# Value products of an attention and gating kernel: three full query slices for each head pair, the leftover queries in 64x64 tiles, and new instruction orders

## The chip, the cores and the metric

The kernel runs on one core of one Trainium2 chip. A core has a matrix engine (PE, whose weight loads are listed apart as PEld), three engines for elementwise work (DVE, ACT, POOL) and a queue engine, SP, that starts transfers (DMA); ACT and POOL can start transfers too. Each engine works through its own instructions in the order in which they stand in the program, and semaphores make one engine wait for another. The metric is the device time of one execution in microseconds, here the median of three runs.

## The reference, cut to what matters

```python
# q, k, v: (8, 12, 448, 64)
scores = scale * q @ k.T                       # for each of 8 x 12 heads, 448 x 448
m = max(scores, axis=-1); e = exp(scores - m)
attn = e / (sum(e) + exp(-m) + 1e-9)
x = (attn @ v) put together as (8, 448, 768)
proj = x @ w_proj                              # 768 -> 3 * 768
x1, x2, x3 = the three parts of proj
x2 = irfft(rfft(x2, axis=1) * rfft(filter_fft, axis=0))   # along the sequence
out = (x1 * x2 * x3) @ w_out
```

## The kernel before, in words

Exponentials are taken without the maximum, so the divisor is the sum of the exponentials plus 1. A flag tells at the end whether a divisor overflowed, and a branch would then do everything again in a safe way; it isn't taken here.

The work is one long list of tasks, each on one engine, with the tokens that it needs and makes (`add(engine, cost, want, emit, need=, make=, ...)`). A class `Plan` replays the list with its own costs (the numbers in `add`, `LANDING`, `DELAY`, `SWITCH` and others) and emits the tasks in the order of that replay. `plan.ORDER` holds one rank for each task, `plan.BANK` the PSUM banks, `plan.FLIP` those tasks that go to their other engine (`alt`). The order of every engine is therefore a table of numbers. On PE, `fill` puts matmuls on a tile of zeros (`idle`) into spare time of the first 40 us, and `spin` puts some at the very start.

**Attention.** The 12 heads of a batch are 6 head pairs, numbered `i`; two pairs, `lead` (even) and turned (odd), make a block, 24 blocks in all. Keys are cut into three tiles of 128 and a rest of 64.

- `scores(t)`: for t = 1 to 3, four matmuls in 64x64 tiles of the array (two heads by two halves of a key tile), 448 queries wide. `t = 0` does the rest keys of both pairs of a block together.
- `exps(t)`: one activation (ACT) of 128x896 for each; it writes `e` (one of `NE` buffers) or `er` (rest keys, one buffer).
- Value products. The queries stand as weights (up to 128 of them), and `vn` (values with a column of ones, 65 wide) streams. The two pairs of a block share one PSUM bank for each head: 2 x 448 queries are 7 slots of 128. Slot 3 is shared: its first 64 rows are the last 64 queries of `lead`, its other rows the first 64 queries of the turned pair.
  - `out_rest(u)`: the products of the three full key tiles for head `u`, on the whole 128x128 array. Every pair goes through four slices, 4 x 3 = 12 matmuls for each head. The slice in slot 3 is half zeros, which is why `e` has 64 columns of zeros (`pads`) around its 448.
  - `out_rests()`: the rest keys with `er`, 14 matmuls in 64x64 tiles for each pair, for `lead` two more on zeros.
  - Two row halves of the array must not write to one bank at the same time. `lead` writes from one half, the turned pair from the other, so `seen` stands between them: a tiny operation (POOL memset `sinks`, in the first 6 blocks ACT copy `sink`) that waits for the first matmuls of `lead`'s `out_rests`, and for which the turned pair's `out_rests` waits.
- `norm` (DVE) adds 1 to the sums, inverts them and scales, into `xb`.

**Inputs.** Batches 0 and 1 (`staged`) are transposed on PE (`k_turn`, `q_turn`) and copied to `kT` and `qT` by DVE or ACT. The later batches (`loaded`) are cast on POOL and transposed by DMA (SP). The rest keys of batches 0 and 1 are transposed three pairs of columns at a time, one beside each second `k_turn` (`turn0` for the first).

**Dense part.** The projections (L1285, L1187, L1169), the transforms (L1235, L1239, L1331) and the output projection (L1103) are matmuls 113 to 452 wide on the whole array, put between the attention's by `ORDER`.

```python
need=[("e", i), ("ones", b % 2), ("v", i), ("vr", b)] + ([("seen", lead)] if turned else [])   # out_rests before
need=[("ER", i), "pads"] + ([("VU", lead, u)] if turned else [])                               # out_rest before
```

## Time and profile before

| | us |
|---|---|
| median of 3 runs | 367.22 |
| the runs | 367.07, 367.22, 370.21 |
| span of the profiled execution, first to last instruction | 367.4 |
| ACT busy in that span | 240.9 (66%) |
| DVE busy | 275.3 (75%) |
| POOL busy | 129.3 (35%) |
| q loads on the SP queue, issue to landing (median) | 4.2 |
| q loads on the POOL queue, issue to landing (median) | 7.8 |

Of the profiled execution the page gives the span, not a device time of its own; the span is 0.2 us over the median of the runs. In rows of the timeline, the first number is the start in us from the beginning of the span, the second the time from the first start to the last end of the instructions that the row puts together (`x8`: eight of them). In rows of groups, the numbers behind the bar are the busy time in us and the mean ns of one. A matmul's own duration of 190 to 350 ns is mostly its way through the array: the next one starts before it ends, so what a matmul costs PE is the distance from its start to the next start.

### The profile page before, as it was taken

What the parts mean: (1) busy time and instruction counts of PE and PEld (TensorE: products, weight loads), DVE (VectorE), ACT (ScalarE), POOL (GpSimd) and SP (SyncE); (2) the same over time, 40 slices, a digit from 0 to 9 for tenths busy, and PEclk for the clock granted to TensorE, in tenths of its full rate; (3) what the DMA queues carried; (4) which work ended last, traced back from release to release, by engine and by line L of the source; (5) the groups of instructions that cost most, each with busy time, mean ns of one, the idle gap of its engine ahead of it and who ended that gap; (6) DMA issues with size and microseconds to landing.
All of it is one profiled execution on the core that took longest, in us unless ns stands there. A gap on an engine that the chain in (4) does not pass through costs nothing. (4 is left out here: it accounts for less than half of the span.)

```text
span 367.4 us, 10725 instructions
## 1 busy us (share of the span) xinstructions
PE 357.2 (97%) x4312; PEld 214.9 (59%) x4312; DVE 275.3 (75%) x667; ACT 240.9 (66%) x388; POOL 129.3 (35%) x278
## 2 busy tenths in 40 slices
PE   8989999999999999999999999999999999999994
PEld 7665675556665556565655555666555655555652
DVE  5468659983799935986499868796468897779970
ACT  5998877756569478667774667877776552333442
POOL 9976243444636463365624525412100100000000
PEclk9999999999999999999999999999999999999999
DMA  8999999986999999999999999986730163125035
GB/s 164 186 191 205 200 221 176 232 178 148 156 224 143 276 188 171 298 233 191 208 165 240 160 188 227 256 203 137 158 70 3 36 189 68 45 53 163 3 132 172
DMA packets 130822, 61.14 MB, mean 166 GB/s; under 512 B 102029, under 2 KB 127568, under 8 KB 130768
## 3 DMA queue, kind: packets, MB, share of 16 engines
q1 hardware_dynamic: 108416, 47.93, 60.9%
q0 software_dynamic: 22112, 12.26, 26.0%
q8 instruction: 34, 0.56, 0.6%
q10 hardware_dynamic: 240, 0.23, 0.2%
q14 instruction: 20, 0.16, 0.2%
HBM read 43.86 MB, written 11.01 MB: 149 GB/s over the span
## 5 line engine op out<-in xcount | busy, mean ns | idle before, releaser
L978 ACT ACTIVATE e<-psum 128x896 bf16<-128x896 f32 x144 | 126.7, 921 | 35.8 <-PE psum L959 32.2
L1285 PE MATMUL psum<-xT,wproj_bf 128*128 128x448 bf16 x576 | 121.5, 353 | 0.1
L1285 PEld LDWEIGHTS <-wproj_bf 128*128 128x128 bf16 x576 | 53.4, 98 | 48.0 <-issue 5.0
L1103 PE MATMUL psum<-wout_bf,yT 128*128 128x384 bf16 x288 | 54.5, 326 | 0.3 <-DVE yT L1373 0.3
L959 PE MATMUL psum<-qT,kT 64*64 64x448 bf16 x576 | 45.5, 360 | 2.0 <-DVE xb L1024 0.8
L1009 PEld LDWEIGHTS <-e 128*128 128x128 bf16 x1152 | 42.0, 98 | 9.1 <-issue 5.1
L1009 PE MATMUL psum<-vn,e 128*128 128x65 bf16 x1152 | 46.7, 194 | 0.0
L1187 PE MATMUL psum<-xf,wproj_bf 128*128 128x452 bf16 x216 | 46.4, 356 | 0.0
L1253 DVE TENSOR_TENSOR t<-xs,hrs 113x768 bf16<-113x768 bf16 (+1 forms) x64 | 38.3, 609 | 4.1 <-ACT xs L498 3.5
L745 POOL CAST nat<-nat 112x512 bf16<-112x512 f32 x36 | 24.3, 681 | 40.6 <-DMA nat<-in_q_dram 40.5
L1300 DVE TENSOR_TENSOR g<-x,psum 128x448 bf16<-128x448 bf16 x48 | 29.2, 615 | 12.0 <-PE psum L1285 11.4
L498 ACT CAST x<-psum 128x448 bf16<-128x448 f32 (+1 forms) x44 | 22.9, 525 | 22.7 <-PE psum L1285 12.5
L1103 PEld LDWEIGHTS <-yT 128*128 128x128 bf16 x288 | 26.7, 98 | 18.7 <-DVE yT L1373 1.1
L498 ACT COPY osb<-psum 128x384 f32<-128x384 f32 x42 | 19.8, 485 | 19.9 <-PE psum L1103 15.0
L771 POOL CAST nat<-nat 128x384 bf16<-128x384 f32 x36 | 21.9, 611 | 26.8 <-DMA nat<-in_k_dram 26.4
L1187 PEld LDWEIGHTS <-wproj_bf 128*128 128x128 bf16 x216 | 19.8, 96 | 19.0 <-issue 1.1
L498 ACT CAST xs<-psum 112x384 bf16<-112x384 f32 (+1 forms) x43 | 20.1, 483 | 13.9 <-PE psum L1235 11.9
L1024 DVE TENSOR_TENSOR xb<-psum,den 128x896 bf16<-128x896 f32 x24 | 26.2, 1092 | 0.8
L959 PEld LDWEIGHTS <-kT 64*64 64x64 bf16 x576 | 15.8, 105 | 16.9 <-issue 12.5
L1259 DVE TENSOR_TENSOR yh<-t 113x384 bf16<-113x384 bf16 (+1 forms) x64 | 24.8, 404 | 0.6
L978 ACT ACTIVATE er<-psum 128x896 bf16<-128x896 f32 x24 | 22.2, 926 | 4.3 <-PE psum L964 4.3
L498 ACT CAST cr<-psum 128x452 bf16<-128x452 f32 x35 | 18.0, 539 | 10.2 <-PE psum L1331 9.7
(143 smaller groups left out, 491.6 us busy)
## 6 DMA issues: line engine op xcount, KB each, us to landing
nat<-in_q_dram SPq DMA_DIRECT2D x37, 224.0 KB, 4.2
out_dram<-osb SPq DMA_DIRECT2D x21, 384.0 KB, 3.8
nat<-in_k_dram SPq DMA_DIRECT2D x38, 192.0 KB, 4.3
nat<-in_v_dram POOLq DMA_DIRECT2D x15, 192.0 KB, 6.2
wproj_bf<-in_moe_w_proj_dram POOLq DMA_DIRECT2D x2, 1152.0 KB, 17.8
out_dram<-osb SPq DMA_DIRECT2D x12, 192.0 KB, 2.8
ks<-in_v_dram POOLq DMA_DIRECT2D x9, 192.0 KB, 5.3
rests<-in_k_dram SPq DMA_DIRECT2D x32, 48.0 KB, 4.1
```

Of the source, the lines that this page charges most:

```text
L498: nc.scalar.copy(to, of)
L745: lambda hp=hp, qsrc=qsrc: nc.gpsimd.tensor_copy(qn[:, hp].rearrange("p j (u d) -> p u j d", u=2), qsrc.rearrange("p (u j d) -> p u j d", ...
L959: nc.tensor.matmul(sc[r, u, 0:S], kT[b % 2][c, hp // 2, 3 * turned + t, r], qT[b % 2][c, hp, :])
L978: nc.scalar.activation(to, of, AF.Exp, scale=SCALE)
L1009: nc.tensor.matmul(out_bank(u)[:, n + 3 * turned, :], P["e"][1 + t][:, o : o + 128], vn[b % 2][:, hp, 4 * u + t, :], start=False, stop=tur ...
L1024: nc.vector.tensor_tensor(W["xb", b][:, hp // 2].rearrange("p s (u d) -> p u s d", u=2), op[:, :, :, 0:DH], rec[:].unsqueeze(3).to_broadca ...
L1103: nc.tensor.matmul(ops[:n, :DCH], y[:, dt, 0:n], wout_bf[:, dt, ch * DCH : (ch + 1) * DCH], start=(dt == 0), stop=(dt == NDT - 1),)
L1187: nc.tensor.matmul(pps, wproj_bf[:, kt, D + dt * 128 : D + (dt + 1) * 128], W["xf", b][:, :, kt, 0:FQ], start=(kt == 0), stop=(kt == NDT - 1),
L1253: nc.vector.tensor_tensor(t[:K], L["xs", par, ch][:K], h, op=ALU.mult)
L1259: nc.vector.tensor_tensor(yh[:K, par, n, ch * DCH : (ch + 1) * DCH], t[:K, 0, :], t[:K, 1, :], op=(ALU.subtract, ALU.add)[n],)
L1285: nc.tensor.matmul(p[:, :S], wproj_bf[:, kt, 2 * part * D + dt * 128 : 2 * part * D + (dt + 1) * 128], xT()[:, kt, 0:S], start=(kt == 0), ...
L1300: nc.vector.tensor_tensor(g[:, dt, :], L["x1", dt], p[:, :S], op=ALU.mult)
```

## The change

1. `out_rest(u)` goes through three slices for each pair: slots 0 to 2 for `lead`, 4 to 6 for the turned pair, 9 matmuls for each head, no zeros. It no longer waits for `out_rests`; it starts the bank itself.
2. `out_rests` does slot 3 as well: six pairs of 64x64 matmuls more (three key tiles, two halves of the slot, two row halves), which read `e` of both pairs. It has 26 matmuls, no dummy ones, waits for the exponentials of both pairs, and `lead`'s waits for `lead`'s `out_rest`. The buffers `e` come free when both are done; there are 9 of them where there were 7.
3. `seen` waits for the last matmuls of `lead`'s `out_rests` and stands on POOL or DVE, never on ACT.
4. `pads` (14 POOL memsets) goes; the rest keys of batches 0 and 1 are transposed by one task each (`rest_turn`, `rest_back`); q and k casts of the first two pairs may stand on either of POOL and DVE; the first q load goes from ACT's queue to SP's, and a tiny first transfer on POOL's queue goes; `SPIN` is 29 where it was 38.
5. The replay's numbers (landings, delays, durations of transfers, a third mode `tall` for the transposes) are others, and `ORDER`, `BANK` and `FLIP` are new throughout.

```diff
-    LANDING = 1.89
-    DELAY = (0.87, 1.6)
+    LANDING = {"SP": 2.0, "POOL": 2.9}
+    DELAY = (0.8, 1.56)
-    SPIN = 38
+    SPIN = 29
-    NE = 7
+    NE = 9
-    es = [const.tile([128, 3 * 64 + 2 * S], BF16, name=f"e{i}") for i in range(NE)]
+    es = [const.tile([128, 2 * S], BF16, name=f"e{i}") for i in range(NE)]
-    plan.ORDER = (9, 2, 6, 1373, 8, 10, 1, 5, 13, 18, ...
...
-                        (nc.sync if g else nc.scalar).dma_start(
+                        nc.sync.dma_start(
...
-            def turn0():
-                nc.tensor.transpose(bank2(("hy", "T0"))[:, 0:128], ks[:, 0, :], ident_bf)
+            def rest_turn():
+                for m in range(NHP // 2):
+                    nc.tensor.transpose(bank2(("hy", ("Tr", b)))[:, 128 * m : 128 * m + 128], ks[:, m, :], ident_bf)
...
         def out_rests():
-            for k in range(PER + 1 - turned):
+            begun = set()
+
+            def beside(s, d, r, e, v, last=False):
+                m = nc.tensor.matmul(out_bank(r ^ turned)[64 * d : 64 * d + 64, s, :], e, v, start=False, stop=bool(last and P.get(("all", r ^ turned)))).ins
+                if not turned:
+                    P["last", r, d] = m.name
+                elif (r, d) not in begun:
+                    begun.add((r, d))
+                    tc.add_manual_dep(m, P["seen"], SYNC, reason="same bank from the other rows")
+
+            for k in range(PER):
                 s, d = divmod(k + PER * turned, 2)
                 for r in range(2):
                     c = slice(64 * r, 64 * r + 64)
-                    m = nc.tensor.matmul(
-                        out_bank(r ^ turned)[64 * d : 64 * d + 64, s, :], P["e"][0][c, 64 * k : 64 * k + 64] if k < PER else idle[c, 0:64],
-                        vn[b % 2][c, hp, 3, :], start=not turned and k < 2, stop=False,
-                    ).ins
-                    if not turned:
-                        P["first", r, d] = m.name
-                    elif k < 2:
-                        tc.add_manual_dep(m, P["seen"], SYNC, reason="same bank from the other rows")
+                    beside(s, d, r, P["e"][0][c, 64 * k : 64 * k + 64], vn[b % 2][c, hp, 3, :])
+            for k in range(6):
+                t, d = 1 + k // 2, (k + 1 - turned) % 2
+                for r in range(2):
+                    c, u = slice(64 * r, 64 * r + 64), r ^ turned
+                    o = S * u + 384 * (1 - d)
+                    beside(PER // 2, d, r, T[lead + d]["e"][t][c, o : o + 64], vn[b % 2][c, hp - turned + d, 4 * u + t - 1, :], k > 3)
-        def seen():
-            at = (nc.gpsimd.memset(sinks, 0.0) if i // 2 in AFAR else nc.scalar.copy(sink, one[0:1, 0:1])).ins
+        def seen(e):
+            at = (nc.gpsimd.memset(sinks, 0.0) if e == "POOL" else nc.vector.memset(sink, 0.0)).ins
...
-                    tc.add_manual_dep(at, P["first", r, d], SYNC, reason="same bank from the other rows")
+                    tc.add_manual_dep(at, P["last", r, d], SYNC, reason="same bank from the other rows")
         def out_rest(u):
-            for n in range(NST):
+            for n in range(3):
                 for t in range(3):
-                    o = 64 + 512 * u + 128 * n - 64 * turned
+                    o = S * u + 128 * n + 64 * turned
                     nc.tensor.matmul(
-                        out_bank(u)[:, n + 3 * turned, :], P["e"][1 + t][:, o : o + 128], vn[b % 2][:, hp, 4 * u + t, :],
-                        start=False, stop=turned == 1 and n == NST - 1 and t == 2,
+                        out_bank(u)[:, n + 4 * turned, :], P["e"][1 + t][:, o : o + 128], vn[b % 2][:, hp, 4 * u + t, :],
+                        start=not turned and n == t == 0, stop=turned == 1 and n == t == 2 and "rests" in P,
                     )
...
-        add("PE", 0.138 if turned else 0.148, w, out_rests, need=[("e", i), ("ones", b % 2), ("v", i), ("vr", b)] + ([("seen", lead)] if turned else []), make=[("ER", i)],
-            take=[("op", i // 2)], give=[("er", (i, 0))], mode="half", mm=16 - 2 * turned)
+        both = [lead, lead + 1]
+        add("PE", 0.227, w, out_rests,
+            need=[(x, j) for j in both for x in ("e", "v")] + [("e0", lead), ("ones", b % 2), ("vr", b)] + ([("seen", lead)] if turned else [("VU", i, 0), ("VU", i, 1)]),
+            make=[("ER", i)] + [("V", j) for j in both], take=[("op", i // 2)], give=[("er", (i, 0))] + [("e", (j, t)) for j in both for t in range(1, 4)], mode="half", mm=26)
...
-        first = tp.tile([1, 16], BF16, name="first")
-        add("POOL", 0.64, -18.5, lambda: nc.gpsimd.dma_start(first, moe_w_out[0:1, 0:16]), need=["ident"], dma=0.05)
...
-        add("POOL", 1.1, 7.0, pads, make=["pads"], after=6.5)
```

Over PE's whole order there are 1152 whole-array value products before and 864 now, 720 matmuls of 64x64 with 65 columns before and 1248 now, and 672 score matmuls in both. Between whole-array matmuls, 64x64 tiles and the transposes' half-width tiles, the shape of the array changes 181 times before and 164 times now.

The first place is on PE, in the middle of the program, at the 11th block. `er0` holds the exponentials of the rest keys, `e4` to `e6` (now `e0` to `e2` and `e6` to `e8`) those of the key tiles of one pair, `vn1` the values, `idle` zeros. Before, from the last rest product of `lead` on:

```order
L989 MATMUL psum_115<-vn1_94,er0_103 64x65
L989 LDWEIGHTS idle_124
L989 MATMUL psum_115<-vn1_94,idle_124 64x65
...
L959 LDWEIGHTS kT1_90
L959 MATMUL psum_115<-qT1_92,kT1_90 64x448
...
L1009 LDWEIGHTS e4_100
L1009 MATMUL psum_115<-vn1_94,e4_100 128x65
L1009 LDWEIGHTS e5_101
L1009 MATMUL psum_115<-vn1_94,e5_101 128x65
```

Now, from the same matmul on; 12 score matmuls (L958 and L963) stand between the two runs of L987:

```order
L987 MATMUL psum_117<-vn1_94,er0_105 64x65
L987 LDWEIGHTS e0_96
L987 MATMUL psum_117<-vn1_94,e0_96 64x65
...
L987 MATMUL psum_117<-vn1_94,e8_104 64x65
L958 LDWEIGHTS kT1_90
L958 MATMUL psum_117<-qT1_92,kT1_90 64x448
...
L963 MATMUL psum_117<-qT1_92,kT1_90 64x448
...
L987 LDWEIGHTS er0_105
L987 MATMUL psum_117<-vn1_94,er0_105 64x65
```

What moved: the leftover queries' products stand behind the rest keys' in the same run of 64x64 tiles, the runs of `lead` and of the turned pair stand on both sides of scores, and the whole-array products of a block stand ahead of them or behind them.

The second place is ACT's order at the start of the program, from its first copy out of PSUM on. `kT0` and `qT0` are the transposed keys and queries, `fr` a table for the filter, `e` and `er0` exponentials. Before:

```order
L498 COPY kT0_89<-psum_115 128x384
L978 ACTIVATE e1_97<-psum_115 128x2x448
L978 ACTIVATE e0_96<-psum_115 128x2x448
L866 CAST fr_84<-psum_115 113x452
L867 ACTIVATE fr_84<-psum_115 113x226
L978 ACTIVATE e2_98<-psum_115 128x2x448
L978 ACTIVATE e3_99<-psum_115 128x2x448
L978 ACTIVATE e4_100<-psum_115 128x2x448
L978 ACTIVATE er0_103<-psum_115 128x896
```

Now:

```order
L498 COPY qT0_91<-psum_117 128x448
L977 ACTIVATE e0_96<-psum_117 128x896
L977 ACTIVATE e1_97<-psum_117 128x896
L498 COPY kT0_89<-psum_117 128x384
L977 ACTIVATE e2_98<-psum_117 128x896
L498 COPY kT0_89<-psum_117 128x384
L977 ACTIVATE e3_99<-psum_117 128x896
L977 ACTIVATE e4_100<-psum_117 128x896
```

What moved: `fr` stands behind the 25th exponential now, and up to the 22nd exponential ACT has only two copies besides, where it had eight operations.

The third place is POOL's order around `seen` (`sinks`), in the attention of the later batches; `nat` and `ks` are staging rooms, and what a row waits for stands in brackets (DMAHW and DMASW are landings). Before, at the 13th block:

```order
L771 CAST nat_105<-nat_105 128x2x3x64 [waits DMAHW7_49]
L745 CAST nat_105<-nat_105 112x2x4x64 [waits DMAHW6_49,DMAHW5_49]
L771 CAST nat_105<-nat_105 128x2x3x64 [waits DMAHW7_49,DMAHW3_49]
L999 MEMSET sinks_114 1x1 [waits PE_49,Pool_49]
L766 DMA nat_105<-in_v_dram 128x4x192 [waits Pool_49]
```

Now, at one of the 14 places where `seen` stands on POOL (10 stand on DVE):

```order
L782 COPY vn0_93<-nat_107 128x3x64 [waits DMASW4_49,PE_49]
L782 COPY vn0_93<-nat_107 128x3x64
L744 CAST nat_107<-nat_107 112x2x4x64 [waits DMAHW5_49,DMAHW1_49]
L744 CAST nat_107<-nat_107 112x2x4x64 [waits DMAHW3_49]
L1008 MEMSET sinks_116 1x1 [waits PE_49]
```

What moved: `seen` still stands behind casts that wait for landings, and the matmul for which it waits is the last of 26 instead of one of the first four.

More of the change, by code (lines that the diff above doesn't have):

```diff
@@ L331, in fillers @@
                 if free:
-                    room = at - end - (sum(self.SWITCH.values()) if was and half else 0.0)
+                    room = at - end - (self.SWITCH["half"] + self.SWITCH["full"] if was and half else 0.0)
                     full[n] = [min(free)[1], max(0, int(part * room / (0.11 if end < 7.5 else 0.056)))]
@@ L569, in staged @@
                 if alone:
-                    add("ACT" if first else "SP", 0.52 if first else 0.5, -21.0 if first else want + 0.1 * n, load,
-                        make=[("s" + name, g)], after=hold, dma=0.95 if name == "q" else 0.71, run=50)
+                    add("SP", 0.5, -21.0 if first else want + 0.1 * n, load,
+                        make=[("s" + name, g)], after=hold, dma=0.84 if name == "q" else 0.73, run=73 if name == "q" else 44)
                 elif hp % 2 == 0:
@@ L575, in staged @@
                         need = [("c" + w, c - 4) for w in "kq"]
-                    add("POOL", 0.73, want + 0.1 * n, load, need=need, make=[(made, g), (made, g + 1)], after=hold, dma=1.05 if name == "q" else 1.0, run=45)
+                    add("POOL", 0.73, want + 0.1 * n, load, need=need, make=[(made, g), (made, g + 1)], after=hold, dma=0.72 if name == "q" else 1.02, run=45)
                 if hp == 0 and name != "q":
@@ L1586, in spin @@
                 nc.tensor.matmul(t[:, 0:128], idle, idle)
-        add("PE", 4.0, -20.0, spin, mm=SPIN, need=["idle"], make=["spin"], take=[("hy", "spin")], give=[("hy", "spin")])
+        add("PE", 3.1, -20.0, spin, mm=SPIN, need=["idle"], make=["spin"], take=[("hy", "spin")], give=[("hy", "spin")])
         add("ACT", 1.3, -20.0, lambda: nc.scalar.activation(warm, zero1, AF.Sin), need=["zero1"], make=["sine table"])
```

95 lines of the change are left out of this document (46 added, 49 removed).

## The prediction

> **What bounds the kernel now.** I read the page's sums first, then the busy time of each engine by stretch.
>
> ```profile
> span 367.4 us, 10725 instructions
> PE 357.2 (97%) x4312; PEld 214.9 (59%) x4312; DVE 275.3 (75%) x667; ACT 240.9 (66%) x388; POOL 129.3 (35%) x278
> ```
>
> ```profile
> core 0: us, PE busy (x) PEld busy (x) DVE busy (x) ACT busy (x) POOL busy (x), PEclk, DMA share, GB/s
> ...
> 7.60:29.10 21.50, 18.60 (x415) 12.81 (x419) 12.08 (x27) 19.68 (x29) 18.93 (x38) 1.00 1.37 187
> 29.10:76.00 46.90, 46.82 (x637) 29.37 (x636) 37.96 (x94) 37.09 (x61) 19.52 (x36) 1.00 1.26 213
> 76.00:120.00 44.00, 43.58 (x564) 27.35 (x564) 33.89 (x79) 29.76 (x46) 20.98 (x47) 1.00 0.92 161
> 120.00:240.00 120.00, 119.87 (x1432) 68.94 (x1430) 92.16 (x207) 82.74 (x130) 55.27 (x114) 1.00 1.13 216
> 240.00:330.00 90.00, 90.00 (x1007) 52.47 (x1006) 69.28 (x176) 52.92 (x86) 7.67 (x19) 1.00 0.42 94
> 330.00:363.20 33.20, 32.12 (x201) 18.08 (x199) 24.79 (x66) 14.70 (x32) 0.00 (x0) 1.00 0.36 117
> ```
>
> From 29.1 to 363.2 us PE is busy for 332.4 of 334.1 us at full granted clock (1.00); no other engine passes 81% of a stretch there (DVE, 37.96 of 46.90). PE's own work sets the end, and each us taken from it counts. From 7.6 to 29.1 it is otherwise: ACT has 19.68 of 21.50 and POOL 18.93, PE waits, and part of its 18.60 is filler on zeros. So the change has to be costed in two pieces: PE's work from the fourth block on, and what lets the fourth block start.
>
> **Prices on PE.** A busy time of the groups misleads here, since it counts the way through the array at the end of each run. I take distances between starts, from a stretch without waits.
>
> ```profile
> L1009 PE MATMUL psum<-vn,e 128*128 128x65 bf16 x1152 | 46.7, 194 | 0.0
> L989 PE MATMUL psum<-vn,er 64*64 64x65 bf16 x672 | 14.9, 194 | 0.9 <-issue 0.9
> ```
>
> ```profile
> 182.33 1.29 PE L1285 MATMUL psum<-xT,wproj_bf 128*128 128x448 bf16 x6
> 183.56 0.57 PE L959 MATMUL psum<-qT,kT 64*64 64x448 bf16 x8
> 183.96 0.29 PE L989 MATMUL psum<-vn,er 64*64 64x65 bf16 x14
> 184.19 0.93 PE L1009 MATMUL psum<-vn,e 128*128 128x65 bf16 x24
> ...
> 187.48 0.76 PE L959 MATMUL psum<-qT,kT 64*64 64x448 bf16 x12
> 188.18 0.74 PE L1285 MATMUL psum<-xT,wproj_bf 128*128 128x448 bf16 x3
> ```
>
> One product takes 0.194 us from its start to its end. 24 whole-array ones take 0.93: (0.93 - 0.19) / 23 = 32 ns from start to start. 14 in 64x64 tiles take 0.29: (0.29 - 0.19) / 13 = 7.7 ns, since four tiles work at once. A wide matmul of 448 columns: (0.74 - 0.35) / 2 is about 0.19 (1.29 less a last one of 0.35, over 5, gives the same). Six of them need 1.14, yet the scores behind them start after 183.56 - 182.33 = 1.23: going into 64x64 tiles costs 0.09. Twelve scores in fours of 0.19 need 0.57, and take 188.18 - 187.48 = 0.70: coming out costs 0.13. A change of shape is 0.11 on average.
>
> **The change, PE from the fourth block's first scores on.** Counted in the two orders, this part holds 1044 whole-array products before and 792 now: 252 x 32 ns = 8.1 us less. It holds 630 of the 64x64 ones before (dummies on zeros included) and 1144 now: 514 x 7.7 ns = 4.0 more. The shape changes 146 and 136 times: 10 x 0.11 = 1.1 less. The table matmul for the filter (0.2) and eight transposes (0.4) now come after this point: 0.6 more. Sum -4.6.
>
> The 7.7 ns is the term with an open side: no row before has 64x64 tiles that add three times to one place, 31 ns apart. The nearest rows are the whole-array products, which add three times to one slot at 32 ns without delay. Between 7.7 and 32 (one after another) I take 7.7, because weights, width and the turn of the four tiles are those of the x14 row. The weight loads that come with each matmul lie inside the measured runs.
>
> A rule of the Trainium skill speaks against this price. "TensorE: Matmul & The Clock Gate", section "Back-to-back issue gap", gives 1 to 64 columns about 60 cycles, a floor of about 25 ns for each matmul. By it the 514 would cost an estimated 12.9 us, and this part would grow by 4.3. The trace's 7.7 ns for 64x64 tiles does not agree, and the measurement decides.
>
> **The start.** Up to the 22nd exponential (the fourth block's first), ACT runs nearly without a pause.
>
> ```profile
> L978 ACT ACTIVATE e<-psum 128x896 bf16<-128x896 f32 x19 | 16.5, 928 | 1.6 <-PE psum L959 1.3
> ...
> L866 ACT CAST fr<-psum 113x452 bf16<-113x452 f32 x1 | 0.5, 543 | 0.0
> L498 ACT COPY xT<-psum 128x448 bf16<-128x448 bf16 x1 | 0.5, 538 | 0.0
> L498 ACT COPY qT<-psum 128x448 bf16<-128x448 bf16 x1 | 0.5, 532 | 0.3 <-DVE kT L500 0.3
> L999 ACT COPY sink<-one 1x1 bf16<-1x1 bf16 x3 | 0.5, 177 | 0.0
> L498 ACT COPY kT<-psum 128x384 bf16<-128x384 bf16 x1 | 0.5, 487 | 0.0
> L867 ACT ACTIVATE fr<-psum 113x226 bf16<-113x226 f32 x1 | 0.4, 362 | 0.0
> ```
>
> ```profile
> 1.26 0.46 SPq L549 DMA_DIRECT2D nat<-in_q_dram  x1
> ...
> 5.30 0.33 DVE L882 TENSOR_SCALAR ft<-sb,half 113x452 bf16<-113x452 bf16 x1
> ...
> 7.12 0.48 ACT L498 COPY kT<-psum 128x384 bf16<-128x384 bf16 x1 [1.02 <-PE psum L636]
> 7.65 0.57 PE L959 MATMUL psum<-qT,kT 64*64 64x448 bf16 x8 [0.34 <-ACT kT L498]
> 8.27 0.92 ACT L978 ACTIVATE e<-psum 128x896 bf16<-128x896 f32 x1 [0.68 <-PE psum L959]
> ```
>
> ```profile
> 29.06 0.28 PE L989 MATMUL psum<-vn,er 64*64 64x65 bf16 x10 [0.89 <-issue]
> 29.15 0.57 PE L959 MATMUL psum<-qT,kT 64*64 64x448 bf16 x8
> ```
>
> Between the first and the 22nd exponential ACT also does 0.54 + 0.36 (`fr`) + 0.54 + 0.53 + 3 x 0.18 + 0.49 = 3.0 us. In the new order two copies of 0.49 stand there: -2.0. The work put off must be done later, when ACT has 20% spare; the same holds for what goes from ACT to DVE. The bounds are 0 (POOL or the landings hold the blocks back instead) and -2.4, PE's own relief before this point, counted the same way; I take -2.0, since ACT's row is the one without idle time. The last wait before the fourth block is one of 0.89 us on nothing that the profile shows ("issue"); I leave it in both sums.
>
> The first exponential itself (8.27): `ft` (0.33) goes out of DVE's queue ahead of the casts, the first q load starts one SP issue later (0.46). Bounds -0.8 (the table matmul and filler ahead of the transposes go too) and +0.5; I take -0.2. The 14 POOL memsets lie ahead of POOL's first loads, so these start some 2 us earlier; on POOL and its queue that is slack, not path. Filler and `SPIN` fill waits and cost nothing; if the waits go, the filler is in the way by its 56 ns each. `rest_turn` and `rest_back` replace as many columns of transposes and copies.
>
> **The new wait.** `seen` now follows the last of `lead`'s 26 matmuls, and behind it in PE's queue, when the turned pair's run isn't cleared, everything waits: scores, and so ACT.
>
> ```profile
> 77.14 0.31 PE L989 MATMUL psum<-vn,er 64*64 64x65 bf16 x14
> 77.27 0.20 PE L989 MATMUL psum<-vn,idle 64*64 64x65 bf16 x2
> ...
> 77.55 0.09 POOL L999 MEMSET sinks<- 1x1 bf16 x1 [1.52 <-PE psum L989]
> ```
>
> With POOL free: the last matmul ends 0.19 after its start (77.47), `sinks` starts at 77.55 and ends at 77.64, and PE starts 0.05 after what releases it (the kT copy's end, 7.60, to 7.65 above): 0.42 us. In the new order the cover between the two runs is one four of scores (0.19) in one block, two fours (0.38) in 9, and 0.5 us or more in 14. Sum 0.23 + 9 x 0.04 = +0.6; bounds 0 (a DVE memset may come back sooner) and +8, when POOL is late (below).
>
> Together: -4.6 - 2.0 - 0.2 + 0.6 = -6.2; 367.4 - 6.2 = 361.2. The span is 0.2 over the median of the runs, so the forecast for the median is **361.0 us**. Transfers move the same bytes, in other order; PE leaves 1.7 us of waits after 29.1, of all causes, so none of them was late before, and none gets 2% earlier demand in a stretch without slack that the profile shows.
>
> **The rivals.** *`seen` late on POOL* (the one on the other side). Once before, it was: the rest products ended at 154.6, `sinks` came at 159.07, behind casts for whose load POOL had waited.
>
> ```profile
> 154.31 0.28 PE L989 MATMUL psum<-vn,er 64*64 64x65 bf16 x13
> ```
>
> ```profile
> 157.84 0.83 POOL L745 CAST nat<-nat 112x512 bf16<-112x512 f32 x1 [6.22 <-DMA nat<-in_q_dram]
> 158.62 0.50 POOL L771 CAST nat<-nat 128x384 bf16<-128x384 f32 x1
> 159.07 0.09 POOL L999 MEMSET sinks<- 1x1 bf16 x1
> ```
>
> That is 4.5 us, with 0.4 of cover now some 4.1 on the path. 14 of the 24 still stand on POOL, most of them behind such casts. One such event leaves 365.1, two 369.2, three 373.3: from 1.5 on the gain is gone. Against it: the order puts them where it expects POOL to be done, and most came 0.1 to 0.3 us after the run. Chance 0.10, half of it within 1% of before.
>
> *64x64 products one after another* (the floor of the Trainium skill, as a mechanism here). At the 32 ns of the whole-array ones the 514 cost 16.4 in place of 4.0: 361.2 + 12.4 = 373.6. The x14 row speaks against it. Chance 0.02.
>
> *Only PE's later part counts.* The start stays bound by POOL, loads or "issue", and small new waits come with the longer holding of `e`, which is freed by whole blocks: -4.6 + 0.6 + 1 = 364.4. POOL's 18.93 of 21.50 speaks for it, the memsets gone from POOL against it. This is also how the change would fail to do what it says, an order that gives back part of its work as waits. Chance 0.15.
>
> *More.* The "issue" wait and the small waits of the first 30 us go too (0.89, and about 1 more of PE's 2.9 idle): 359.2. Chance 0.10.
>
> *The forecast*, 361.0 within about 1.3, has 0.63.
>
> **Numbers.** A measurement of this kernel tells about 1% from no change. Faster by over 1% (below 363.5) takes the forecast, "more" and half of "only the later part": 0.81. Within 1%: the other half and half of late `seen`, 0.13. Slower: 0.06. The range that leaves out about two in ten reaches from 358.8, near "more", to 364.6, "only the later part".
>
> **What would show it.** PE's products 864 and 1248 strong, at 32 and 8 ns from start to start; the fourth block's scores at about 27 instead of 29.15; from there to the last matmul 329.5 instead of about 334; no wait of over 0.3 us ahead of the turned pair's rest products. Wrong if those waits sum to over 2 us, if 64x64 starts lie over 12 ns apart, or if the fourth block starts no earlier.

## The result, and the profile after

The changed kernel takes 373.03 us (median of 4 runs, 371.03 to 373.3), the kernel before beside it 367.53 (367.07 to 370.21): a ratio of 1.0128, with a 95% interval of 1.009 to 1.0166. (The two medians alone would give 1.015.) The forecast was 361.0 with a range up to 364.6. The change makes the kernel about 1.3% slower. All ratios below are to runs of the kernel before on the same chip, with their 95% intervals. Executions over 1.5% slower than the fastest of their kernel are left out of the ratios, which matters for one kernel, after_fewer_rows, where that takes seven of twelve, so that its ratio (1.0013) and its median over all (372.86) do not belong together.

The page's sums of the changed kernel (its profiled execution took 373.3 us, with a span of 371.5):

```profile
span 371.5 us, 11195 instructions
PE 352.6 (95%) x4564; PEld 209.9 (56%) x4564; DVE 272.8 (73%) x685; ACT 238.7 (64%) x376; POOL 120.6 (32%) x258
```

PE was busy for 357.2 us and is now for 352.6, yet the span has grown from 367.4 to 371.5. Wherever a run has both on record, its time is 1.7 to 1.9 us above its span. So the profiled execution of the kernel before, with a span of 367.4, took about 369.2 us by this, more than the median of 367.22, and the two traces lie closer together (4.1 us) than the medians (5.5). The changed kernel's groups of value products, with busy time, mean ns of one, idle time before them and what ended it:

```profile
L1018 PE MATMUL psum<-vn,e 128*128 128x65 bf16 x864 | 37.6, 194 | 0.0
L987 PE MATMUL psum<-vn,er 64*64 64x65 bf16 x672 | 14.8, 197 | 0.0
L987 PE MATMUL psum<-vn,e 64*64 64x65 bf16 x576 | 13.9, 192 | 0.5 <-issue 0.5
```

864 whole-array products and 1248 in 64x64 tiles stand there, as forecast. Busy time by stretch, with the columns of the prediction's table:

```profile
core 0: us, PE busy (x) PEld busy (x) DVE busy (x) ACT busy (x) POOL busy (x), PEclk, DMA share, GB/s
7.60:29.10 21.50, 19.55 (x473) 13.24 (x473) 12.12 (x34) 19.63 (x25) 17.46 (x34) 1.00 1.36 187
29.10:76.00 46.90, 45.30 (x650) 29.00 (x651) 38.48 (x97) 34.66 (x57) 20.00 (x42) 1.00 1.15 193
76.00:120.00 44.00, 42.22 (x593) 26.01 (x590) 32.52 (x77) 30.22 (x46) 23.13 (x48) 1.00 1.05 196
120.00:240.00 120.00, 113.39 (x1464) 64.08 (x1461) 89.65 (x213) 75.78 (x115) 50.89 (x107) 1.00 1.12 213
```

Before, PE left 0.08, 0.42 and 0.13 us idle in the last three of these stretches. Now it leaves 1.60, 1.78 and 6.61. The clock is full (1.00) in all of them.

To put work and waits apart I priced PE's matmuls by their distances, as the prediction did: 32 ns, 7.7 ns, 0.19 us for 448 columns (for four of them in 64x64 tiles), by the same reading 0.16 for 384, 0.195 for 452 and 0.05 to 0.06 for 113 and 128 (about half of that for the transposes in half-width tiles), 0.11 for a change of shape, nothing for matmuls on zeros. The sum is 344.2 us of work before and 337.6 after, 6.6 less. The prices are those of the prediction, so this sum tests its counts. What is left of the time up to a given moment is time in which PE did no work:

| up to (us) | 16 | 29 | 40 | 76 | 120 | 140 | 220 | 352 |
|---|---|---|---|---|---|---|---|---|
| before | 9.9 | 12.8 | 13.3 | 14.2 | 15.6 | 15.7 | 16.1 | 17.1 |
| after | 11.0 | 13.2 | 15.5 | 16.2 | 19.2 | 23.8 | 27.1 | 28.2 |

So the counts came true, and 11.1 us of waits ate it: about 2 up to 40 us, and 9 from there to the end, nearly all of it between 76 and 220. What PE waited for from 76 to 240 us, in the chain of releasers (us in total, times, longest us), first in the kernel before, then in the changed one:

```profile
PE psum L1103 <- DVE yT L1373: 0.3, 1, 0.3
```

```profile
PE psum L958 <- DMA qT<-nat: 3.4, 2, 2.7
PE psum L1200 <- DVE g L1313: 1.9, 1, 1.9
PE psum L958 <- DMA kT<-nat: 0.9, 1, 0.9
PE psum L1116 <- DVE yT L1386: 0.9, 1, 0.9
PE psum L958 <- ACT ldm L498: 0.7, 1, 0.7
PE psum L1344 <- DVE g L1313: 0.4, 1, 0.4
```

Half of it is scores that wait for a transposed q or k. The longest such wait, first on the queue of SP, then on PE (start, duration, idle time before):

```profile
119.77 1.96 SPq L758 DMA_DIRECT2D nat<-in_k_dram  x2
121.83 1.30 SPq L705 DMA_TRANSPOSE qT<-nat  x1
```

```profile
129.08 0.38 PE L958 MATMUL psum<-qT,kT 64*64 64x448 bf16 x4 [2.66 <-DMA qT<-nat]
...
134.91 1.47 PE L1116 MATMUL psum<-wout_bf,yT 128*128 128x384 bf16 x8 [0.94 <-DVE yT L1386]
```

As a whole the transposes of q are not much slower than before (median from issue to landing 5.0 us, before 4.8): they are asked for closer to their use. From the landing of a transposed q or k to its first scores, for pairs 12 to 23, the kernel before has 2.1 to 8.8 us wherever the trace has both ends. The changed one has under 0.1 us at three of them, where PE stood still for two, and 0.6 at a fourth, and is late at a fifth, the one above. At that one both things came together: if its landing ended the wait, it took 129.08 - 121.83 = 7.25 us, more than any other transposed q of this trace (6.2 at most). With the median of 5.0 the wait would have been about 0.4 us. An order without slack turns such scatter into waits.

### The profile page after: what moved, and what is told of

Same layout as the page of the kernel before. It is cut to its first block, busy times and chain, and to the rows that moved or that the text cites. A ratio compares the mean times of both kernels' runs of the same rounds, so it can differ in the third digit from the quotient of the medians.

```text
span 371.5 us, 11195 instructions
## 1 busy us (share of the span) xinstructions
PE 352.6 (95%) x4564; PEld 209.9 (56%) x4564; DVE 272.8 (73%) x685; ACT 238.7 (64%) x376; POOL 120.6 (32%) x258
## 5 line engine op out<-in xcount | busy, mean ns | idle before, releaser
L958 PE MATMUL psum<-qT,kT 64*64 64x448 bf16 x576 | 44.6, 357 | 6.3 <-DMA qT<-nat 3.4
L498 ACT CAST x<-psum 128x448 bf16<-128x448 f32 (+1 forms) x48 | 25.1, 528 | 30.1 <-PE psum L1298 17.0
L744 POOL CAST nat<-nat 112x512 bf16<-112x512 f32 x36 | 23.4, 650 | 48.1 <-DMA nat<-in_q_dram 48.0
L1018 PEld LDWEIGHTS <-e 128*128 128x128 bf16 x864 | 33.9, 98 | 8.2 <-issue 1.6
L1018 PE MATMUL psum<-vn,e 128*128 128x65 bf16 x864 | 37.6, 194 | 0.0
L1266 DVE TENSOR_TENSOR t<-xs,hrs 112x768 bf16<-112x768 bf16 (+1 forms) x64 | 35.3, 570 | 0.9 <-issue 0.3
L498 ACT CAST xs<-psum 112x384 bf16<-112x384 f32 (+1 forms) x42 | 19.8, 484 | 16.9 <-PE psum L1248 12.8
L498 ACT COPY osb<-psum 128x384 f32<-128x384 f32 x40 | 18.7, 484 | 14.6 <-PE psum L1116 11.5
L770 POOL CAST nat<-nat 128x384 bf16<-128x384 f32 x36 | 19.3, 545 | 26.2 <-DMA nat<-in_k_dram 26.1
L958 PEld LDWEIGHTS <-kT 64*64 64x64 bf16 x576 | 15.1, 105 | 21.8 <-issue 14.6
L1272 DVE TENSOR_TENSOR yh<-t 112x384 bf16<-112x384 bf16 (+1 forms) x64 | 23.6, 393 | 0.7 <-DVE t L1266 0.5
```

The source lines that it names most:

```text
L498: nc.scalar.copy(to, of)
L744: lambda hp=hp, qsrc=qsrc: nc.gpsimd.tensor_copy(qn[:, hp].rearrange("p j (u d) -> p u j d", u=2), qsrc.rearrange("p (u j d) -> p u j d", ...
L958: nc.tensor.matmul(sc[r, u, 0:S], kT[b % 2][c, hp // 2, 3 * turned + t, r], qT[b % 2][c, hp, :])
L1018: nc.tensor.matmul(out_bank(u)[:, n + 4 * turned, :], P["e"][1 + t][:, o : o + 128], vn[b % 2][:, hp, 4 * u + t, :], start=not turned and ...
L1266: nc.vector.tensor_tensor(t[:K], L["xs", par, ch][:K], h, op=ALU.mult)
L1272: nc.vector.tensor_tensor(yh[:K, par, n, ch * DCH : (ch + 1) * DCH], t[:K, 0, :], t[:K, 1, :], op=(ALU.subtract, ALU.add)[n],)
```

## The experiments

The first theory was *late feeds*: the new order asks for transfers later or uses them sooner, and what PE saves turns into waits for them. The rivals: less PE work does not become time in any order; the order as a whole, whatever resource is late, has lost its margin; and, later, a cost in the products themselves.

**Does less PE work become time at all?** before_three_slices is the kernel before with the fourth slice of `out_rest` left out (288 whole-array products, 9.2 us of PE's work), its order unchanged.

```diff
-            for n in range(NST):
+            for n in range(NST - 1):
```

> The kernel before, in its own order, with a quarter of its out_rest products left out (12 -> 9 of each 12; the last query slice of every pair is not summed): 288 products of 32 ns, 9.2 us of PE work less, and nothing else moved. Theory 'feed' (the changed kernel's order starts the loaded batches' transfers late and uses them without slack; PE work saved under another order shows): 358 to 361 us. Rival 'transfers bound any order' (PE work saved anywhere between 60 and 240 us turns into waits for transfers, in the order of before too): 364 to 367. Rival 'products' (the new way of the value products brings the waits itself): it says nothing against 358 to 361 here.

362.69 us, ratio 0.9863 (0.9829 to 0.9897): 5.6 us by medians, between the two theories. In the old order saved PE work still becomes time, at about 60% (by the interval of the ratio, 3.8 to 6.3 us of 9.2); a 1.5 us wait on POOL for `sinks` is new. The other way round, after_twelve adds a fourth, repeated slice to the changed kernel (9.2 us of work).

```diff
-            for n in range(3):
+            for m, n in enumerate((0, 1, 2, 2)):
```

> The changed kernel with its third full query slice multiplied twice (12 products in each out_rest in place of 9; that slice's sums come out doubled): 288 products of 32 ns, 9.2 us of PE work more, in the changed order. About half of the blocks lie between 60 and 220 us, where PE waits 11 us for transfers. Theories 'feed' and 'transfers bound any order': the half that lies there is done in time in which PE waited anyway, 376 to 379 us. Rival 'products' (PE's own work sets the time throughout): all 9.2 us show, 381 to 383 us.

380.71 us, ratio 1.029 (1.0213 to 1.0367), about 1.6% or 6 us over the changed kernel, between the two theories again. By these figures a third of the added work vanished in waits that were there already, but the two intervals together allow 3 to 9 us of the 9.2. PE's work counts in both kernels; that it counts for less than its full price is shown for the kernel before alone.

**Which transfers?** after_wout_later moves one load (the output weights, which POOL starts) behind the first two q casts of batch 2 in POOL's order; after_sp_moves moves five entries of SP's queue so that transposes come earlier.

```diff
+    at = list(plan.ORDER)
+    for n, rank in ((364, 247),):
+        at[n] = rank
```

> The changed kernel with the load of wout (2.36 MB, landed 20.6 us after its issue at 43.8 us) moved behind the first two q casts in POOL's queue, so that the first loaded q and k no longer share the DMA engines with it. Theory 'feed': SP's first transposed q is issued at 54 to 57 instead of 60.6 us, and of the waits at 86, 108 and 129 us (4.7 in all) half or more goes: 368 to 371 us, if wout itself is not late at 73 us. Rival 'transfers bound any order': 372 to 374. Rival 'products': 372 to 374.

```diff
+    for n, rank in ((121, 117.5), (156, 220), (159, 240), (175, 289), (740, 549),):
```

> The changed kernel with five of SP's 180 steps moved a few places forward in SP's queue, no work changed: the transposed q of pair 14, of pairs 18-20 and of 21-23, the transposed k of 18-20, and the transposed x of pairs 28 and 29, whose landings ended PE waits of 0.9, 1.1, 2.7 and 2.1 us (6.8 in all). Theory 'feed': most of the 6.8 goes, 366 to 369 us. Rival 'transfers bound any order': what was moved back is late in its place, 371 to 374. Rival 'products': no change, 372 to 374.

They gave 372.4 (1.0139, 1.0113 to 1.0166) and 371.58 (1.0101, 1.0059 to 1.0143): nothing, and perhaps 1 us. In after_wout_later SP's first transposed q is issued at 57.85 us in place of 60.61, and its trace, which is of its fastest execution (369.71), has 1.8 us of waits for q and k in place of 4.3 from 76 to 240 us; its median shows no gain. In after_sp_moves the waits for q and k from 76 to 240 us fall from 4.3 to 0.7 us, and others stand in their place, for the transposed `x` and for `sinks` (its line numbers are 4 higher):

```profile
PE psum L1252 <- DMA x<-ldm: 1.7, 2, 1.1
PE psum L991 <- POOL sinks L1012: 1.0, 1, 1.0
PE psum L962 <- DMA qT<-nat: 0.7, 1, 0.7
```

Next the loads of the rest keys and values were left out from batch 3 on (40 of 64 small transfers on SP), in both kernels.

```diff
-        for i in range(4):
+        for i in range(4 if b < 3 else 0):
```

> The changed kernel without the loads of the last 64 k and v rows (rests) for batches 3 to 7, which leaves those rows of batch 2 in their place: 40 DMAs of 48 KB less, each group of four about 2.6 us of SP's queue, six groups between 87 and 147 us. Theory 'feed' and rival 'transfers bound any order': SP's queue runs several us earlier from 87 us on, the waits at 98, 108 and 129 us go, 366 to 370 us. Rival 'products': 372 to 374, since PE's own work is what it was.

> The kernel before without the same 40 loads of the last k and v rows of batches 3 to 7 whose removal made the changed kernel 6 us faster. Theory 'feed': the order of before has its inputs in time, only some 2 us of waits stand between 60 and 220 us in its trace, so 366 to 368.5 us beside 368 for the kernel before. Rival 'transfers bound any order': transfers hold the kernel before too, 362 to 365 us.

The changed kernel gains 6 us: 367.18 (0.9961, 0.9925 to 0.9998). The kernel before gains 1 at most: 368.07 beside 369.52 (0.9978, 0.9945 to 1.0011). So the changed kernel does wait for transfers, or for the room in SP's queue that these 40 took, and the old one doesn't, as *late feeds* has it. after_light and before_light go further: no q and k loads from batch 3 on either.

```diff
-                lambda hp=hp, qsrc=qsrc: nc.sync.dma_start(
+                lambda hp=hp, qsrc=qsrc: b < 3 and nc.sync.dma_start(
```

The load of k gets the same condition, and the rests are left out as above.

> The changed kernel without the loads of q, k and the last k and v rows of batches 3 to 7 (30 q, 30 k and 40 rests DMAs of SP's 233; the rows of batch 2 stand in their place; casts, transposes and everything on PE as they were). With the transfers out of the way PE's own work shows. Theory 'feed': the waits of 8 us between 76 and 240 us go, 362 to 365 us, and 3 to 6 us below before_light, of the 6.6 us that PE's products and changes of shape save by their spacing. Rival 'products' (the new way of the value products brings the waits by itself, through its longer hold of the e tiles and of the out banks): 369 to 373 us, above before_light.

> The kernel before with the same loads left out, as the measure for after_light. Theory 'feed': it waits for hardly any transfer, 366 to 368 us, within 2 us of the kernel before. Rival 'transfers bound any order': 362 to 365 us.

371.49 (1.0062, 1.0031 to 1.0092) and 370.76 (1.0046, 1.002 to 1.0071): with nearly all those loads gone the changed products are still no faster than the old ones, and *late feeds* alone falls. The time lies where the rival, a cost in the products themselves, put it. The waits don't show its mechanism, a longer hold of `e` and of the output banks: PE waits 0.2 us for exponentials. It waits 3.1 us on "issue", which is the subject of the last experiments, and otherwise mostly for DVE (from the waits of after_light):

```profile
PE psum L1116 <- DVE ldm L500: 1.7, 1, 1.7
PE psum L1116 <- DVE yT L1386: 1.6, 1, 1.6
PE psum L908 <- issue: 0.9, 1, 0.9
PE psum L1344 <- DVE g L1313: 0.8, 1, 0.8
```

POOL's casts no longer wait for data there and move together: from 120.4 to 133.7 us it has no pause over 0.3 us. That this is what makes DVE late is argued, not shown.

**The order.** after_slack and after_margin are the changed kernel with orders from a new search in a replay of the program, the one with all transfers landing 1.6 us later, with some scatter, and lasting 4% longer, the other with landings that scatter as the traces show and a limit on how fast PE's program comes in. before_margin is the control: the kernel before, its own order searched again in the second way. after_before_order starts from the order of the kernel before and is searched so. Only the tables change.

```diff
-    plan.ORDER = (0, 5, 1, 10, 15, 6, 2, 3, 7, 11, 12, 160, 4, 20, 2
+    plan.ORDER = (5, 1, 2, 2, 3, 1, 0, 0, 1, 3, 0, 10, 0, 4, 6, 1, 8
```

> The changed kernel's work, banks and tiles, with the order (and the engine of steps that have two) searched anew from the changed kernel's own, on replays in which every transfer lands 1.6 us later than the planner's figure and by an amount that varies from one to the next, and lasts 4% longer, instead of on one exact replay. Theory 'feed' (the changed order asks for inputs with no slack, and another order of the same work has it): the waits between 60 and 220 us, 11 us in the changed kernel's trace, fall by half or more, 363 to 368 us. Rival 'transfers bound any order': the waits move and stay, 371 to 374 us.

> The changed kernel's work in an order searched once more from after_slack's, on replays in which transfers land later by amounts spread as in the traces so far (about 1 us either way, transposes of x 0.5 to 0.9 us later) and PE's program is taken in at 6.1 us per 256 rows during the first 46 us, as the issue waits of the traces show it. Theory 'feed': the issue waits (4.7 us in after_slack) and the waits for transfers both fall, 362 to 367 us. Rival 'transfers bound any order': 371 to 375 us, the waits stand elsewhere again.

> The kernel before in an order searched from its own in the same way and for as long as after_margin's. It tells what the search itself is worth, where nothing is short of time. Theory 'feed': 366 to 369 us, within 1% of the kernel before, since its transfers were in time already. If it comes out faster by more than 1% the search and not the changed products would explain a gain of after_margin; if it comes out slower, the replays miss something that also holds the changed kernel's orders back.

> The changed kernel's products, tiles and e buffers in the order of the kernel before: every step that both kernels have stands where it stood before, the rest products of a block are moved behind both of its out_rest steps as they must, and a search then moved steps by a few places, on replays with transfers up to 1.6 us later. Theory 'feed' (the loss is in when the changed order asks for its inputs): transposed q and k land 2 us or more ahead of their first use as in the kernel before, and 362 to 366 us. Rival 'products' (the new way of the value products costs the waits in any order): 371 to 374 us.

| | us | ratio | interval |
|---|---|---|---|
| after_slack | 376.57 | 1.0165 | 1.0106 to 1.0223 |
| after_margin | 370.85 | 1.0093 | 1.0062 to 1.0124 |
| before_margin | 372.46 | 1.0135 | 1.01 to 1.017 |
| after_before_order | 370.09 | 1.0038 | 1.0002 to 1.0074 |

The control tells most: a new order from a replay makes the *old* products 1.35% slower, as much as the change did. (That search isn't the one that made the changed kernel's order, so it tells what a new order can cost, not what this one did.) None of the four came where *late feeds* had it: after_slack is slower than either theory said, the other three lie 3 to 4 us above the range of *late feeds*. The trace of before_margin has the same kind of small waits (76 to 240 us):

```profile
PE psum L959 <- DVE ldm L500: 1.0, 1, 1.0
PE psum L959 <- DMA qT<-nat: 0.9, 1, 0.9
PE psum L959 <- DMA kT<-nat: 0.5, 1, 0.5
PE psum L989 <- POOL sinks L999: 0.3, 1, 0.3
```

At equal searching the changed products are 0.4% faster than the old ones (1.0093 against 1.0135, intervals that overlap), where the work alone would give 1.8%. after_before_order comes nearest to the kernel before, but it did not keep the old margins: PE waits 1.1 us for a transposed k, and 1.2 us each for `sinks` and on "issue".

after_raw_order is the test without any search: the changed products with the old order carried over by hand, each `out_rests` behind the old places of its predecessors.

```diff
-    plan.ORDER = (0, 5, 1, 10, 15, 6, 2, 3, 7, 11, 12, 160, 4, 20, 2
+    plan.ORDER = (9, 2, 6, 8, 10, 1, 5, 13, 18, 20, 70, 118, 3, 14, 
```

> The changed products with the order of the kernel before carried over by hand and not searched at all: every task that both kernels have keeps its rank, bank and engine; lead's out_rests stands right behind the later of the turned pair's old out_rests and lead's second out_rest, the turned pair's out_rests right behind its own second out_rest, and seen at the first place on POOL or DVE (POOL from the seventh block on) that is free by then. If the search on replays buys nothing real, and a late order is made of the scatter on the chip: no slower than the searched version of it (ratio 1.0038), so 0.990 to 1.004, 365 to 370 us, with the margins of before's transposed inputs back and waits only where out_rests now follows the turned pair's exponentials. If the change itself costs the time, by holding e and the output banks longer whatever the order: slower than the searched version, 1.006 to 1.025, 371 to 377 us, with waits of PE on ACT's exponentials, on e's release or on seen in most blocks.

380.17 us, ratio 1.0313 (1.0277 to 1.0349): the other theory's side, and beyond its range. But its waits (7.6 to 363 us) are not those of the changed kernel:

```profile
PE psum L987 <- POOL sinks L1008: 3.5, 4, 1.6
PE psum L1018 <- issue: 2.2, 2, 1.4
PE psum L1589 <- issue: 1.1, 1, 1.1
```

No wait for a transfer above 0.2 us is left, and the smallest time from landing to use for q and k, where the trace has both, is 3.6 us: the late inputs belong to the new order, not to the new products (though this kernel is also slower, which gives its transfers time). What it loses is something else, and in the old order it is the products' own: 224 changes of shape, where the kernel before has 177 and the changed one 162 (47 x 0.11 = 5.2 us, so that its work is 345.2 us, no less than before), 3.5 us for `seen`, and "issue". The arithmetic gain needs PE's order to be written anew, and what was written anew lost its margin.

**The waits on nothing.** In every run so far with the changed products PE waits 1.2 to 4 us between 20 and 42 us on "issue", nothing that the profile shows; those of the kernel before have 0 to 0.9. In the changed kernel and in after_raw_order:

```profile
33.53 0.32 PE L908 MATMUL psum<-uw,fr 113*112 113x384 bf16 x1 [0.93 <-issue]
...
40.02 0.28 PE L987 MATMUL psum<-vn,e 64*64 64x65 bf16 x10 [0.45 <-issue]
```

```profile
23.86 0.19 PE L1018 MATMUL psum<-vn,e 128*128 128x65 bf16 x1 [0.82 <-issue]
30.08 0.89 PE L1589 MATMUL psum<-idle 128*128 128x128 bf16 x13 [1.10 <-issue]
36.57 0.19 PE L1018 MATMUL psum<-vn,e 128*128 128x65 bf16 x1 [1.36 <-issue]
```

From each of these waits to the next the trace counts 128 matmuls and 128 weight loads, and they are 6.2 to 6.5 us apart. That looks like a program that arrives in pieces of 256 rows, one each 6.3 us in this stage (25 ns a row, 50 for a matmul with its weights), with PE waiting where it uses them faster. The traces bear it out: they hold the transfers that bring the program, packets of 16 KB on a queue called "q8 instruction". In the changed kernel such packets end at 32.06 and 38.50 us, and PE goes on at 33.53 and 40.02. Of the 36 waits on "issue" between 16 and 46 us, in all eighteen traces, each ends 1.2 to 1.7 us behind the end of such a packet. A packet is under way for about 0.9 of the 6.3 us in the changed kernel; where the rest goes isn't shown.

The changed products need more rows for less work, ten products a block. Two kernels add rows to the kernel before, 64x64 products on zeros in the first six blocks (the edit shown is that of before_rows_40; before_rows_10 has 5 for 20); one takes rows from the changed kernel by leaving out five of six added pairs in `lead`'s `out_rests` there.

```diff
-            for k in range(PER + 1 - turned):
+            for k in [*range(PER + 1 - turned)] + [PER] * (20 if i < 12 and not turned else 0):
```

> The kernel before, with ten 64x64 products on zeros more for each of the first six blocks (as many as the change adds there, net, and at the same place). On PE they are 10 x 7.8 ns a block, 0.5 us in all. In the program they are 20 rows a block, a matmul and a weight load each. If PE is limited between 17 and 42 us by how fast its program comes (about 6.2 us for 256 rows, 24 ns a row), the four blocks in that stage cost 80 rows, 1.9 us: waits of PE on nothing that the profile shows (issue) of 1.5 to 2.8 us in place of 0.9, and 1.0 to 2.5 us more time, a ratio of 1.003 to 1.007. If only PE's work counts: issue stays at about 0.9 and the ratio is 1.000 to 1.002.

> The same with forty products more for each of the first six blocks: 1.9 us of PE's work in all, and 80 rows a block. If the supply of the program limits: 320 rows in the four blocks between 17 and 42 us are 7.7 us, of which what lies in waits that are there already costs nothing: issue waits of 3 to 7 us, 5 to 8 us more time, a ratio of 1.013 to 1.022. If only PE's work counts: issue at about 0.9, 1.9 us more, a ratio of 1.004 to 1.006.

```diff
-            for k in range(6):
+            for k in range(6 if turned or i >= 12 else 1):
```

> The changed kernel, with five of the six added pairs of 64x64 products left out of lead's out_rests in the first six blocks (10 products, 20 rows and 0.08 us of PE's work a block), so its output isn't the reference's. If the supply of the program limits: issue waits of 0 to 0.5 us in place of 1.4, and by 40 us about 2 us less time lost than in the changed kernel; the ratio to the kernel before 1.005 to 1.010, by as much as the later waits don't take it back. If only PE's work counts: issue at about 1.4, the ratio 1.010 to 1.014.

before_rows_10: 370.29 us, 1.0047 (1.0019 to 1.0074). The ratio is in the supply theory's range, yet the trace has the same 0.9 us of "issue" as before, where that theory had 1.5 to 2.8: one sign for it, one against. before_rows_40: 377.42 us, 1.0248 (1.0209 to 1.0287), 9 us for 1.9 us of PE's work and above the range of 1.013 to 1.022. From 16 to 46 us it waits:

```profile
PE psum L959 <- issue: 1.7, 1, 1.7
PE psum L989 <- issue: 1.4, 2, 0.9
```

From 16 to 45 us the time without counted work grows by 8.9 us, in the kernel before by 3.3; of the 5.6 more the added products explain 1.3 and the longer "issue" waits (3.1 in place of 0.9) 2.2. Most of the rest fits a clock at half speed right behind the longest of these waits, which ended at 30.74 us (the clock is the column behind POOL's):

```profile
31.90:35.30 3.40, 3.40 (x89) 2.99 (x85) 0.66 (x2) 2.42 (x5) 1.32 (x2) 0.51 1.17 212
```

Half the clock for 3.4 us takes up to 1.7 us of PE's work. Another 2.5 us were lost before 16 us and have nothing to do with the added rows, which come later: PE waited 2.3 us for DVE, four operations of which took 2.42 us beside POOL memsets (in the kernel before 0.92), and its clock was then at 0.50 from 8.1 to 11.5 us. So of the 9 us of this run some 4 belong to the rows, their half clock included, besides the work of 1.9. after_fewer_rows has no "issue" wait left in that stage:

```profile
PE psum L958 <- ACT e L977: 0.3, 1, 0.3
```

Up to 40 us its time without work is 13.6 us, in the changed kernel 15.5, in the kernel before 13.3: the 2 us lost there were program rows. Its times, 366.18 to 376.24 us, scatter too far to tell whether the whole got faster. From 40 to 352 us it still loses 11.2 us, like the changed kernel (12.7) and unlike the one before (3.8).

## Why the prediction was wrong

- *PE's work*: right. 6.6 us less were counted in the trace, of which the forecast had 4.6 from the fourth block on and the rest ahead of it. The prices held too: whole-array products in a run still start 32 ns apart, and the 64x64 products that add three times to one place are no slower than the others, from the timeline of PE:

```profile
28.48 0.32 PE L987 MATMUL psum<-vn,er 64*64 64x65 bf16 x14
28.61 0.29 PE L987 MATMUL psum<-vn,e 64*64 64x65 bf16 x12
28.71 0.38 PE L958 MATMUL psum<-qT,kT 64*64 64x448 bf16 x4
```

  These 26 take 0.23 us from their first start to the scores behind them, 9 ns each, a little over the 7.7 of the price. The floor of about 25 ns that the Trainium skill gives in "TensorE: Matmul & The Clock Gate", section "Back-to-back issue gap", does not hold for four tiles in turn.
- *The start, -2.0 - 0.2*: right, though not for the whole reason given. ACT has only its two copies between the exponentials, the first exponential starts at 7.96 us (before 8.27), the 22nd at 27.58 (before 29.57), and the 22nd group of scores at 26.53, where "about 27" was forecast. ACT's row was called the one without idle time; the row itself has 1.6 us of it.
- *From there to the last matmul*: wrong, by 10 us. It starts at 366.24 us in place of 362.13, so this part grew from 333.0 to 339.7 us. The forecast was 329.5.
- *"The last wait before the fourth block is one of 0.89 us on nothing that the profile shows ("issue"); I leave it in both sums"*: too small. That wait was the sign of a limit which the change tightens, rows of program. The text priced what the products cost PE's array and counted no rows. They cost about 1.8 us between 29 and 40 us, and after_fewer_rows, with fewer rows, loses 1.9 us less up to 40.
- *The new `seen` wait, +0.6*: right, in mechanism and in size. PE's own rows show no such wait, because each is shorter than the way of the scores ahead of it through the array. The weight loads show nine, from the waits of the changed kernel:

```profile
PEld L987 <- POOL sinks L1008: 2.3, 8, 0.3
PEld L987 <- DVE sink L1008: 0.3, 1, 0.3
```

  Counted from start to start, with 0.19 for each four of the scores ahead, PE lost about 0.7 us at these nine places (up to 0.18 each). *`seen` late on POOL*, with its 4 us and more, did not come. In other orders it is what is late (3.5 us in after_raw_order).
- *"None of them was late before, and none gets 2% earlier demand in a stretch without slack that the profile shows"*: this is the step that failed, with some 9 us (27.1 - 15.5 from 40 to 220 us, where the kernel before loses 16.1 - 13.3). Small waits showed that the old order had enough margin. They said nothing of the margins of a new order, and the diff replaced all of it. The transposed q and k, which had 2.1 us or more before, had under 0.1 at three places; half of the waits listed from 76 to 240 us are for them, and the rest for DVE and ACT. The margins were to be had: the order tells which transpose stands how far ahead of its scores, the trace how long one takes.
- *"Only PE's later part counts", an order that gives back part of its work as waits*, had a chance of 0.15 and 1 us for those waits. Its mechanism came, though not at the start, and its size was 9 us.

What is shown: the waits that took back the saved work, one by one, in the changed kernel's trace; the old order, carried over as it is, takes the changed products without waiting for a transfer, though it then loses more by other things; the old products lose 1.35% in an order from a new search; transfers are part of the loss (6 us gone with the rest loads), but not a part that stays put, since with more loads gone DVE is late in their place. The products themselves cost something in any order tried: 1.2 to 4.0 us of waits for program rows, where the old ones have 0 to 0.9. What stays open: how much of the 9 us a better order could get back. The best that was run, after_before_order, is at 1.0038 and not below the kernel before, and a version that beats it was not found. Also open is why a replay with scattered landings still picks orders that lose on the chip.

## What to carry to other kernels

Where PE is 99% busy, its saved work is worth only what the order behind it can feed: before crediting it, take for each transfer the time from its landing to its first use, in the new order with the old trace's durations, and distrust the credit where little is left (here the scatter of one transfer alone cost over 2 us). If a change comes with a new order, price the order by itself, with the old work in an order from the same source as a control. And count instructions as well as cycles: splitting products into more, shorter ones can be limited by how fast the program arrives.

## What was not expected of the hardware

- *Program supply*: 256 rows in 6.2 to 6.5 us between 17 and 42 us, where the DMA engines are busy nearly throughout, with PE's waits ending 1.2 to 1.7 us behind the end of a packet. The page of the changed kernel has the queue; 0.59 MB in 36 packets are 16 KB each, 64 bytes for each of 256 rows:

```profile
q8 instruction: 36, 0.59, 0.7%
```

- *DVE beside POOL*: the `yT` for which PE waited at 134.9 us took 2.14 us, where the 24 of its group take 0.62 on average; POOL went from cast to copy without a pause all that time.

```profile
L1386 DVE TENSOR_TENSOR yT<-g,cv 128x768 bf16<-128x768 bf16 x24 | 14.7, 618 | 0.4
```

```profile
132.71 2.14 DVE L1386 TENSOR_TENSOR yT<-g,cv 128x768 bf16<-128x768 bf16 x1
```

```profile
132.10 0.62 POOL L744 CAST nat<-nat 112x512 bf16<-112x512 f32 x1 [1.98 <-DMA nat<-in_q_dram]
132.66 0.64 POOL L782 COPY vn<-ks 128x192 bf16<-128x192 bf16 x2
133.24 0.62 POOL L744 CAST nat<-nat 112x512 bf16<-112x512 f32 x1
133.80 0.64 POOL L782 COPY vn<-nat 128x192 bf16<-128x192 bf16 x2
134.39 0.96 POOL L782 COPY vn<-ks 128x192 bf16<-128x192 bf16 x2
```

The Trainium skill, "SBUF — State Buffer", section "SBUF: two separate sides", has DVE and GpSimd share a pair of ports by an exclusive lock, held for a whole operation. The trace agrees in that this DVE operation was slow while POOL was at work, but it lasted over several POOL operations, not one.

- *A wait that costs twice*: PE of after_slack waited 2.78 us up to 121.8 us, and the granted clock (the column behind POOL's) was 0.64 in the next stretch; twelve matmuls of 448 columns took 3.70 us there in place of about 2.4.

```profile
122.00:126.00 4.00, 4.00 (x20) 1.71 (x19) 3.93 (x13) 1.73 (x2) 0.61 (x1) 0.64 1.11 217
```

```profile
121.77 0.58 PE L958 MATMUL psum<-qT,kT 64*64 64x448 bf16 x2 [2.78 <-DVE g L1313]
122.28 3.70 PE L1298 MATMUL psum<-xT,wproj_bf 128*128 128x448 bf16 x12
```

Seven such stretches stand in the traces between 7 us and the last matmul: one each in after_slack, after_twelve, after_wout_later, after_no_rests and after_light, and two in before_rows_40. Each lasts 3.4 us at a clock of 0.50 to 0.51 and begins during a wait of 1.4 to 2.8 us or up to 1.2 us behind one. The length of the wait alone doesn't decide it: the changed kernel waited 2.66 us up to 129.08 and kept a clock of 1.00.
